# Linear attention with a gated feed-forward layer on one core: the second batch's q and k transposed by the DMA, half loads, and tail groups that keep their PSUM tile, in a new order

## Chip, cores, metric

One core of one Trainium2 chip. The metric is the device time of one execution, in microseconds (us). The profile names the engines PE (TensorE matmul), PEld (its weight loads), DVE (VectorE), ACT (ScalarE), POOL (GpSimd) and SP (SyncE, which here only issues transfers). A run over 1.5% above the fastest of the same kernel is counted as slow; ratios below use the other runs, called fast, alone.

## The reference

```python
# q, k, v: (8, 8, 576, 64) float32; w_phi: (64, 128)
def phi(x):
    proj = x @ w_phi
    proj = proj - max(abs(proj), over the 128 features)
    return concatenate([exp(proj), exp(-proj)])
q_p, k_p = phi(q), phi(k)
kv, z = k_p^T @ v, sum of k_p over the sequence
x = (q_p @ kv) / (q_p @ z + 1e-6)          # per head; heads side by side: (8, 576, 512)
x_prev = x shifted by one row
xk = mu_k*x + (1-mu_k)*x_prev;   xr = mu_r*x + (1-mu_r)*x_prev
out = sigmoid(xr @ w_r) * (relu(xk @ w_k)**2 @ w_v)      # d_ff = 1024
```

(shortened; all results in float32, the kernel's matmuls in bfloat16)

## The kernel before

Work is cut into 32 head pairs (eight batches of four), numbered through. Each pair goes through projections of q and k, row maxima (`nm`, on DVE), their splitting into two bfloat16 halves (`mhl`), a transposition of these on PE (`ps_m`), exponentials, `kv`, numerator and denominator, and `x_sc`. From pair 8 on, `x_sc` is transposed by a DMA on SP's queue into `xs` (`xz` below), copied by POOL for the shift (`xu`), differenced (`df`) and mixed into `xk` and `xr`. The feed-forward layer of a batch (ps_h, ps_r, ps_v; ps_he, ps_re, ps_ve for the rows that two batches share) then fills PE. The last 64 rows of each head form "tail groups", one for each batch (three for batch 0). A list of names, `ORDER`, fixes the program order of every engine; a name's suffix picks its engine or PSUM slot.

```python
def tr(p0, p1):                                  # q and k of two pairs, transposed by the DMA
    def f():
        t = get(qkT, b, inp, [128, NP * R, 128], BF, "qkT")
        nc.sync.dma_start_transpose(out=t[:, R * p0:R * p1, :],
                                    in_=nat[b][:, p0:p1, :].rearrange("p a x -> p (a x)"))
    return f
...
NPT = 2                                          # batches transposed by PE instead
lparts = {b: [(0, NP)] for b in range(B)}        # whole loads ...
lparts[0] = [(0, 1), (1, 2), (2, 4)]
lparts[1] = [(0, 2), (2, 4)]
...
# tail group: ps_e has two banks, [:, 0] for k and [:, 1] for q
def mte():
    s["pm"] = pm = motile(("mo", "m" + tag), "ps_me")       # a single bank of its own
    nc.tensor.transpose(pm[:, 0:64].bitcast(BF), mh, ident)
def kae():                                                  # add the row maxima of k
    nc.tensor.matmul(s["ps"][:, 0, 0:n * 128], lhsT=s["mT"][0:64, :], rhs=sel[...],
                     start=False, stop=True, skip_group_check=True)
def qte():
    s["pq"] = ps = motile(("mo", "q" + tag), "ps_qe")       # another single bank
    ...
def eqe():                                                  # exponentials tq, out of s["pq"]
    ...
def xz():
    nc.sync.dma_start_transpose(out=xs[:, a, :]..., in_=s["x"]...)
def xu(eng):
    copy(eng, xs[:, a, 1:64], xs[:, a, 576:639])
```

(cuts are marked with dots)

## Time and profile before

| | before |
|---|---|
| time, median of the first 4 runs | 305.4 us (304.2 to 306.4) |
| span of the profiled run | 304.2 us |
| PE / DVE / ACT / POOL busy | 92 / 79 / 73 / 42% |
| first matmul of the feed-forward layer | 51.9 us |
| transposes of xs by the DMA, landing | 3.5 us in the median, 13.4 at most |

The busy shares are averages. Where time is lost is read from the 40 slices, and from "useful work": the number of matmuls of each kind in a stretch times the pitch at which that kind runs when nothing holds it up. The prediction below derives those pitches and shows the lines; in 130 to 140 us the kernel before does 4.8 us of such work, elsewhere after 60 us 8 to 10.

### The profile page before, as it was taken

What the parts mean: (1) busy time and instruction counts of PE and PEld (TensorE: products, weight loads), DVE (VectorE), ACT (ScalarE), POOL (GpSimd) and SP (SyncE); (2) the same over time, 40 slices, a digit from 0 to 9 for tenths busy, and PEclk for the clock granted to TensorE, in tenths of its full rate; (3) what the DMA queues carried; (4) which work ended last, traced back from release to release, by engine and by line L of the source; (5) the groups of instructions that cost most, each with busy time, mean ns of one, the idle gap of its engine ahead of it and who ended that gap; (6) DMA issues with size and microseconds to landing.
All of it is one profiled execution on the core that took longest, in us unless ns stands there. A gap on an engine that the chain in (4) does not pass through costs nothing.

```text
span 304.2 us, 9054 instructions
## 1 busy us (share of the span) xinstructions
PE 278.4 (92%) x3765; PEld 158.4 (52%) x3813; DVE 240.3 (79%) x369; ACT 223.3 (73%) x408; POOL 127.4 (42%) x261
## 2 busy tenths in 40 slices
PE   6688798999899999969999997999999999999993
PEld 2456465565456655534555654454556655554541
DVE  5776789979978999667978988799869888777331
ACT  3397899998689897855888884898797878923410
POOL 7763533696047346653443714353034403400400
PEclk9999989999999999998999999999999999999999
DMA  8999957399989957996957898913924364233125
GB/s 152 204 209 207 169 83 105 59 194 206 194 174 128 148 124 131 197 200 113 177 110 107 145 125 157 162 47 61 187 60 69 11 93 94 58 74 71 39 58 116
DMA packets 66137, 38.18 MB, mean 126 GB/s; under 512 B 47024, under 2 KB 60720, under 8 KB 66096
## 3 DMA queue, kind: packets, MB, share of 16 engines
q1 hardware_dynamic: 51280, 20.82, 39.4%
q0 software_dynamic: 14672, 16.48, 35.1%
q8 instruction: 30, 0.49, 0.7%
q10 hardware_dynamic: 144, 0.29, 0.3%
q14 instruction: 11, 0.09, 0.1%
HBM read 33.62 MB, written 9.44 MB: 142 GB/s over the span
## 4 chain that ended last, share of the span: by engine, by line
PE 61%; DVE 18%; DMA 7%; ACT 6%; issue 3%; POOL 2%; SPq 1%; DVEq 0%; POOLq 0%
PE ps_v L812 14%; PE ps_h L779 13%; PE ps_r L798 7%; PE ps_nd L656 5%; DMA xs<-x_sc 4%; PE ps_kv L635 4%; DVE nm L565 4%; DVE nm L560 3%; DVE xk L706 2%; PE ps_ve L896 2%; ACT q L620 2%; PE ps_he L866 2%; DVE xr L706 2%; PE ps_q L548 2%; PE ps_k L598 2%
## 5 line engine op out<-in xcount | busy, mean ns | idle before, releaser
L620 ACT ACTIVATE q<-ps_qT 128x512 bf16<-128x512 f32 x128 | 67.1, 622 | 3.0 <-PE ps_qT L612 2.8
L575 ACT ACTIVATE k<-ps_k 128x1024 bf16<-128x1024 f32 x64 | 62.9, 1038 | 5.6 <-PE ps_k L598 4.3
L779 PE MATMUL ps_h<-xk,wk_bf 128*128 128x512 bf16 x237 | 60.8, 379 | 1.3 <-issue 0.3
L812 PE MATMUL ps_v<-wv_bf,kk 128*128 128x512 bf16 x243 | 58.2, 379 | 1.0 <-issue 0.3
L565 DVE TENSOR_REDUCE nm<-ps_q 128x8 f32<-128x1024 f32 x32 | 38.7, 1218 | 4.3 <-PE ps_q L548 4.1
L560 DVE TENSOR_REDUCE nm<-ps_k 128x8 f32<-128x1024 f32 x32 | 38.8, 1217 | 3.8 <-PE ps_k L548 3.8
L812 PEld LDWEIGHTS <-kk 128*128 128x128 bf16 x256 | 23.9, 98 | 28.8 <-issue 1.9
L211 POOL TENSOR_TENSOR kk<-krelu 128x512 bf16<-128x512 bf16 x23 | 23.9, 1047 | 35.4 <-DVE krelu L205 21.7
L779 PEld LDWEIGHTS <-wk_bf 128*128 128x128 bf16 x256 | 22.5, 97 | 25.2 <-issue 2.3
L584 POOL CAST mhl<-nm 128x16 bf16<-128x16 f32 x32 | 8.0, 250 | 64.1 <-DVE nm L560 64.0
L798 PE MATMUL ps_r<-wr_bf,xr 128*128 128x512 bf16 x118 | 32.9, 394 | 1.2 <-issue 0.5
L804 ACT ACTIVATE rt<-ps_r 128x512 bf16<-128x512 f32 x32 | 19.5, 609 | 18.0 <-PE ps_r L798 15.7
L700 POOL TENSOR_TENSOR diff<-xs 128x576 bf16<-128x576 bf16 x21 | 28.0, 1336 | 7.6 <-DVE xs L682 2.8
L203 ACT ACTIVATE krelu<-ps_h 128x512 bf16<-128x512 f32 x39 | 23.2, 611 | 10.1 <-PE ps_h L779 8.3
L706 DVE SCALAR_TENSOR_TENSOR xk<-diff,mu_k_t,xs 128x576 bf16<-128x576 bf16 x32 | 28.5, 892 | 1.3 <-POOL diff L700 1.0
L818 DVE SCALAR_TENSOR_TENSOR ob<-rt,ps_v 128x512 f32<-128x512 bf16 x32 | 21.8, 682 | 8.7 <-PE ps_v L812 4.2
L666 DVE TENSOR_TENSOR x_sc<-ps_nd,rden 128x640 bf16<-128x640 f32 x32 | 26.4, 825 | 1.1
L706 DVE SCALAR_TENSOR_TENSOR xr<-diff,mu_r_t,xs 128x576 bf16<-128x576 bf16 x32 | 26.9, 840 | 0.0
L548 PEld LDWEIGHTS <-qkT 64*128 64x128 bf16 x512 | 17.6, 94 | 12.0 <-issue 9.7
L635 PE MATMUL ps_kv<-v,k 64*128 64x65 bf16 x1024 | 22.8, 192 | 0.6 <-ACT q L620 0.4
L635 PEld LDWEIGHTS <-k 64*128 64x128 bf16 x1024 | 19.9, 95 | 5.1 <-issue 3.8
L205 DVE TENSOR_SCALAR krelu<-ps_h 128x512 bf16<-128x512 f32 x25 | 17.1, 688 | 6.6 <-PE ps_h L779 6.0
(99 smaller groups left out, 467.5 us busy)
## 6 DMA issues: line engine op xcount, KB each, us to landing
out_dram<-ob SPq DMA_DIRECT2D x72, 128.0 KB, 2.4
nat<-in_k_dram POOLq DMA_DIRECT2D x6, 576.0 KB, 8.6
nat<-in_q_dram POOLq DMA_DIRECT2D x6, 576.0 KB, 8.9
vt<-in_v_dram POOLq DMA_DIRECT2D x6, 576.0 KB, 9.6
wk_bf<-in_moe_w_k_dram POOLq DMA_DIRECT2D x2, 512.0 KB, 10.8
wv_bf<-in_moe_w_v_dram POOLq DMA_DIRECT2D x2, 512.0 KB, 12.3
nat<-in_k_dram POOLq DMA_DIRECT2D x3, 288.0 KB, 7.4
nat<-in_q_dram POOLq DMA_DIRECT2D x3, 288.0 KB, 7.3
```

Of the source, the lines that this page charges most:

```text
L211: (nc.vector if eng == "DVE" else nc.gpsimd).tensor_tensor(out_, in_, in_, op=ALU.mult)
L560: nc.vector.tensor_reduce(s["nm"][:, 0, :], s["k"].rearrange("p a (g f) -> p (a g) f", f=128), axis=AX.X, op=ALU.max, apply_absolute_value ...
L565: nc.vector.tensor_reduce(s["nm"][:, 1, :], s["q"].rearrange("p a (g f) -> p (a g) f", f=128), axis=AX.X, op=ALU.max, apply_absolute_value ...
L575: nc.scalar.activation(s[f"k{pn}"], s["k"].rearrange("p a (g f) -> p (a g) f", f=128), AF.Exp, scale=(1.0 if pn == 0 else -1.0))
L620: nc.scalar.activation(t[:, h, :].rearrange("f (g a p) -> f g a p", g=4, a=2), s["qT"].rearrange("f a (g h p) -> f h g a p", g=4, h=2)[:, ...
L635: nc.tensor.matmul(ps[:, hh, pn * 65:(pn + 1) * 65], lhsT=s[f"k{pn}"][r, c, :], rhs=vb[r, a, 2 * g + par, :], start=(pn == 0 and c == 0), ...
L666: nc.vector.tensor_tensor(s["x"].rearrange("p (b s) d -> p b s d", b=2), ndv[:, :, :, 0:64], s["rd"].to_broadcast([128, 2, 5, 64]), op=ALU ...
L700: (nc.vector if eng == "DVE" else nc.gpsimd).tensor_tensor(s["d"], xs[:, a, 64:64 + S], xs[:, a, 0:S], op=ALU.subtract)
L706: nc.vector.scalar_tensor_tensor(out=t[:, a, (b % 2) * S:(b % 2 + 1) * S], in0=s["d"], scalar=mu[:, a:a + 1], in1=xs[:, a, 0:S], op0=ALU.m ...
L779: nc.tensor.matmul(ps, lhsT=wk_bf[:, c, fc * 128:(fc + 1) * 128], rhs=xkt[bp][:, c, m0:m0 + 512], start=(c == 0), stop=(c == NDC - 1))
L798: nc.tensor.matmul(ps, lhsT=xrt[bp][:, c, m0 + ci * 128:m0 + (ci + 1) * 128], rhs=wr_bf[:, c, :], start=(c == 0), stop=(c == NDC - 1))
L812: nc.tensor.matmul(ps, lhsT=s["kk"][:, fc, ci * 128:(ci + 1) * 128], rhs=wv_bf[:, fc, :], start=(fc == 0), stop=(fc == NFC - 1))
```

## The change

The intent: free PE, DVE and ACT of the second batch's transposes at the start; keep large loads away from the transposes of x (a half load below brings two of a batch's four pairs); give the tail groups fewer PSUM banks to wait for. The order of nearly everything is new as well.

```diff
-    NPT = 2
-    lparts = {b: [(0, NP)] for b in range(B)}
+    NPT = 1
+    lparts = {b: [(0, 2), (2, 4)] for b in range(B)}
...
+        pace = lambda i: [f"xu{4 * (b - 3) + i + (a0 > 0) * (1 if i > 3 else 2)}"] if b > 4 else []
-            op(f"lk{tag}", "POOL", 0.75, at("lk"), ld(0), ["ident"], alloc=al("nat"), chain="ld")
+            op(f"lk{tag}", "POOL", 0.75, at("lk"), ld(0), ["ident"] + pace(0), alloc=al("nat"), chain="ld")
...
         def mte():
-            s["pm"] = pm = motile(("mo", "m" + tag), "ps_me")
-            nc.tensor.transpose(pm[:, 0:64].bitcast(BF), mh, ident)
+            nc.tensor.transpose(s["ps"][:, 1, 0:64].bitcast(BF), mh, ident)
...
         def qte():
-            s["pq"] = ps = motile(("mo", "q" + tag), "ps_qe")
+            s["pq"] = ps = s["ps"][:, 1, :]
...
-        op("mh" + N, "POOL", 0.5, (K("mh"), n), mhx, ...)
+        op("mh" + N, "POOL", 0.5, (K("mh"), n), mhx, ..., alt=("POOL", "DVE"))
```

(cut; further: one exponential of 1024 columns in place of two of 512 for q, mixes and row-maxima splits that may run on POOL or DVE, one more buffer for some tiles, the last output in two halves, and a new `ORDER`. The k, q and v loads of batches 5 to 7 are each held until a given `xu` has run, by `pace`.)

## The prediction

> **What bounds the kernel now.** I read the page first (busy shares, the 40 slices), then the busy time by stretches, then the chain that ended last, then the groups of instructions, and last the timeline of the worst gap.
>
> ```profile
> PE 278.4 (92%) x3765; PEld 158.4 (52%) x3813; DVE 240.3 (79%) x369; ACT 223.3 (73%) x408; POOL 127.4 (42%) x261
> ...
> PE   6688798999899999969999997999999999999993
> ...
> PE 61%; DVE 18%; DMA 7%; ACT 6%; issue 3%; POOL 2%; SPq 1%; DVEq 0%; POOLq 0%
> ```
>
> TensorE (PE) carries the time, except in three places: the first seven slices (0 to 55 us), one slice near 135 us, and the last one. But 92% flatters it: records of pipelined matmuls overlap. I therefore price its useful work by pitch, read off the chain: four ps_h matmuls in 0.86 us (0.215 each, 512 columns), 20 ps_nd in 0.64, 16 ps_kv in 0.24, 8 projections in 0.22, 9 ps_pt in 0.62. Times the counts of the groups: the 32 head pairs 75 us, the feed-forward 138 + 17 (the joint rows of two batches), tail groups 7, transposes 7, together 245 us of a span of 304.2. The same pricing of the instructions in each stretch gives the PE time lost there (length less useful work, so the fills that only keep the clock up count as lost):
>
> 0 to 55: 29 us lost. 55 to 130: 8 (0.11 per us). 130 to 140: 5.3. 140 to 290: 14 (0.09 per us). 290 to 304.2: 5.0.
>
> ```profile
> core 0: us, PE busy (x) PEld busy (x) DVE busy (x) ACT busy (x) POOL busy (x), PEclk, DMA share, GB/s
> 0.00:55.00 55.00, 43.49 (x708) 27.34 (x714) 41.96 (x79) 40.91 (x81) 30.29 (x67) 0.97 0.98 164
> 55.00:130.00 75.00, 72.95 (x1070) 42.51 (x1082) 65.75 (x93) 63.05 (x115) 40.23 (x73) 1.00 0.98 154
> 130.00:140.00 10.00, 7.07 (x72) 3.46 (x72) 5.58 (x9) 5.82 (x12) 5.58 (x16) 0.83 1.23 198
> 140.00:290.00 150.00, 145.63 (x1883) 81.13 (x1907) 123.28 (x185) 111.77 (x199) 51.34 (x107) 1.00 0.56 95
> ```
>
> Until 55 us DVE and ACT are about three quarters busy and PE has little to do: the feed-forward, its filler, cannot start before pairs 0 to 3 are mixed and wk has landed (first ps_h at 51.9 us). The chain there goes from DVE reductions to PSUM copies and exponentials, so DVE and ACT work is what counts. At 130 to 140 the timeline shows one slow transfer:
>
> ```profile
> 125.10 13.39 DMA xs<-x_sc
> 138.49 0.05 issue
> 138.55 0.23 POOL xs L199
> 138.78 0.04 POOL xs L682
> 138.82 0.14 POOL mhl L584
> ```
>
> GpSimd (POOL) stands at the copy of xs until that transpose lands. The row maxima of the tail group and of the next pairs (mhlt, mhl) are behind such copies in its queue, and PE waits for them (longest 2.4 us); then PE runs at half clock for 3.4 us. Five loads of 576 KB were issued between 117.5 and 126.9 us, just ahead.
>
> **What the Trainium skill says.** "DMA: Bandwidth & Descriptors", Queues, rings and completion order: each DMA engine takes the queues in turn, a whole packet at a time. So a transpose on one queue shares with big loads on another; the trace agrees in kind: xs transposes land in 3.5 us in the median and in 13.4 behind those five loads. "TensorE: Matmul & The Clock Gate", Part 1: an idle window puts the array at half clock for a window of about 3.4 us; the trace shows two such spells, at 36.6 and at 135 us, 3.4 us each, 1.7 us of work lost in each. "GPSIMD Engine Reference", 4.1 Engine selection: two-input elementwise work is about twice as slow as on VectorE; here it is worse, the same difference of 576 columns takes 1336 ns on POOL and 495 on DVE. "Perfetto Trace Analysis", Identifying the Most-Contended Engine, warns of matmul busy time as I found it: 278 us busy for 245 us of work.
>
> **The change part by part.** Lists and diff show a new order of everything, so I count by kind.
>
> (1) Batch 1 by DMA. Gone: 36 of the 72 ps_pt transposes (36 x 0.067 = 2.4 us of PE) and 8 PSUM copies, on DVE 4 x 0.486 + 2 x 0.418 = 2.8 us, on ACT 2 x 0.587 = 1.2 us. New: two transposes of the kind of which 12 exist (landing 5.4 us in the median, 12.8 at worst). They go out while DMA is saturated (the first 30 us run at 0.93 to 1.2 share), but the weights now come after q and k. At 205 GB/s (slices 3 and 4) q and k of batches 0 and 1 with the first halves of v, 2.9 MB as they are listed, are in at about 16 us; even two slow transposes end near 35 us, when pair 4 wants them, so I call them hidden.
>
> (2) Start as a whole. I multiply the instructions listed before the first ps_h by their row's durations: DVE 36.0 us before and 34.5 after, ACT 37.9 and 34.6 (copies gone, one exponential of 1024 columns for two of 512: 0.13 us saved for each pair, four small copies moved; against it mhl, two DVE operations instead of two POOL ones, for five of six pairs). At the same density (36.0/51.9 = 69% and 37.9/51.9 = 73%) ps_h begins at 49.7 by DVE and 47.4 by ACT. I take 48.5: **3.4 us**. The 29 more fills (68 against 39) should keep the clock up near 36 us, which is inside that number.
>
> (3) The hole at 130 to 140. Half loads, for batches 5 to 7 each held back until a given xs copy has run, leave fewer bytes ahead of a transpose; 15 of 32 mhl and 6 of 10 mhlt go to DVE, so a waiting POOL no longer stops PE. The excess is 5.3 - 0.9 = 4.4 us; I count **4**.
>
> (4) Tail groups write row maxima and q's tail into the second bank of their own tile: 20 uses fewer of the two single banks that ps_h, ps_r and ps_v alternate in, against a three-fold tile held about 1.1 us longer (two tq exponentials). With deeper buffers (kpn, qpn, kvs, krelu, rt, d one more each) this goes at the stretches of 180 to 190 and 200 to 210 us, which lose 2.2 and 1.8 instead of 0.9: excess 2.2 us. I count **2**.
>
> (5) The end. The last joint rows come in two halves of 256 columns, the last output on two queues. Now: ps_ve done at 299.25, ob 0.69, two issues in 1.10, landing. Half of ob and of the issues goes: 0.35 + 0.55 = **0.9 us**.
>
> (6) Costs. Some 18 more load issues of 0.75 us on POOL, 13 us of an engine with 58% idle: off the path, unless a copy of xs waits behind one. Five mixes go to POOL, two operations and over 2 us each, chosen where it has time. For new waits in an order made on a model of the machine I take off 0.7.
>
> Sum: 3.4 + 4 + 2 + 0.9 - 0.7 = 9.6 us, and 305.6 - 9.6 = 296. The parts err rather low, as the lists were searched with more freedom (engines, buffers): I say **295**.
>
> **Rivals.** *A, the hole moves*: batches 2 to 4 are not held back, POOL still runs all xs copies in order, and a slow transpose can stop it elsewhere (33.5 us of its waits are on xs). For: 12 such waits exist, only one hurts PE much. Then parts 3 and 4 give 2 instead of 6: 299. *B, the start is bound by DMA*: the transposes of batch 1 and the later weights hold up pair 4 or ps_h. For: DMA full until 30 us. Against: it falls to 0.6 from 40 us on, before ps_h. Then part 2 gives nothing or costs 2: 298 to 301. *C, DVE becomes the bound*: the lists give it 238 us against 239, so its share hardly moves; against. It would show as 300 and more. *D, denser throughout*: losing 0.07 instead of 0.09 per us over 225 us would give 5 us more: 290.
>
> **Range and chances.** A and B together end at about 302, D at 288; eight in ten lie in 288 to 302. Faster by over 2% means under 299.6: only A with B, or C, miss it, so 0.78; same 0.20; slower 0.02.
>
> **What would show it.** Right: first ps_h at 47 to 50 us; no copy of ps_pt for batch 1, ps_pt x36; no half-clock spell after 10 us; no slice of PE under 9 between 60 and 290; xs landing under 8 us at worst; q exponentials x64 at about 1.04 us. Wrong: PE waiting for qkT by DMA before 50 us (B), PE behind mhl or xs once more (A), DVE above 85% after 60 us (C). The prediction falls if the useful-work pricing shows the loss after 60 us unchanged or grown.

## The result

The kernel after is slower. Its first four runs gave 318.7 us in the median (314.4 and 316.8 fast, 320.5 and 321.9 slow), a ratio to the kernel before of 1.034 [1.024, 1.043]. Run once more beside later experiments it gave 318.8 us (317.0 to 320.2, all fast), ratio 1.041 [1.036, 1.047]:

> The kernel after once more, unchanged, for a profile in the fast state and for times on one chip with the other runs of this call. Theory (x transposes in turn with loads): the same holes at 140 to 150 and 200 to 210 us as in the slow profile, useful work below 6 us in each, POOL's waits for xs over 40 us. Rival (the holes belong to the slow state): they are gone in a fast profile. Time of the fast runs 313 to 317.

The holes are in its fast profile too (3.9 and 3.5 us of useful work), and POOL's waits for xs are 51.1 us; only its time is higher than I said. A ratio is the mean time of one kernel's fast runs over that of the other's of the same rounds, so not quite the ratio of the medians quoted; the interval in brackets is of 95%. The lines below are from the fast profile of that second run.

The page of the kernel after (busy shares, two rows of the slices, the chain):

```profile
PE 284.1 (90%) x3761; PEld 158.4 (50%) x3814; DVE 249.5 (79%) x409; ACT 222.3 (70%) x346; POOL 143.6 (45%) x235
...
PE   8798889998999899977999999198999889999995
...
PEclk9999999999999999995999999789999999999999
...
PE 56%; DVE 21%; issue 6%; DMA 6%; POOL 5%; ACT 4%; SPq 0%; DVEq 0%; POOLq 0%; ACTq 0%
```

The hole that was one slice near 135 us is gone from there, but the 19th and the 26th slice (143 to 151 and 198 to 206 us) are new holes, with the clock halved beside each. The stretches around them, first of the kernel after, then the same ones of the kernel before (columns as in the prediction):

```profile
130.00:140.00 10.00, 9.68 (x164) 5.81 (x165) 9.62 (x16) 8.83 (x14) 5.98 (x7) 1.00 1.13 96
140.00:150.00 10.00, 6.24 (x31) 2.70 (x31) 6.43 (x9) 5.71 (x11) 7.52 (x15) 0.69 1.26 223
200.00:210.00 10.00, 5.10 (x30) 2.11 (x32) 8.16 (x12) 3.04 (x6) 5.13 (x7) 0.66 0.81 98
```

```profile
140.00:150.00 10.00, 9.77 (x115) 4.98 (x113) 9.97 (x13) 6.59 (x11) 5.38 (x10) 1.00 0.74 117
200.00:210.00 10.00, 9.44 (x154) 5.19 (x156) 9.58 (x13) 9.23 (x19) 6.22 (x13) 1.00 0.09 19
```

In useful work, in us, summed from the start (matmul counts times pitches, as in the prediction, but without the transposes ps_pt, which the change takes from PE: 4.8 us before and 2.4 after):

| us from start | before | after | difference |
|---|---|---|---|
| 60 | 25.3 | 26.2 | +0.9 |
| 100 | 60.7 | 61.9 | +1.2 |
| 120 | 79.6 | 78.5 | -1.1 |
| 140 | 94.0 | 96.9 | +2.9 |
| 150 | 103.2 | 100.7 | -2.5 |
| 200 | 148.3 | 145.2 | -3.1 |
| 210 | 156.8 | 148.7 | -8.1 |
| 260 | 204.0 | 191.7 | -12.3 |
| 290 | 233.1 | 220.3 | -12.8 |

So the start gained a little, the old hole was filled, and two new holes and a thinner 100 to 110 and 240 to 260 us cost more. How the hole at 200 us comes about is in the chain of the kernel after, in order of time (start, length, what):

```profile
190.32 8.14 DMA xs<-x_sc
198.47 0.05 issue
198.52 0.24 POOL xs L210
198.76 0.04 POOL xs L692
198.80 0.07 issue
198.87 1.28 POOL diff L709
200.15 0.02 issue
200.18 1.57 DVE xk L720
201.75 1.14 DVE xr L720
202.89 1.14 DVE nm L573
204.03 0.02 issue
204.06 0.37 DVE mhl L597
204.43 0.02 issue
204.45 0.18 DVE mhl L598
```

and in the timeline, DVE's and PE's first work after it (in brackets: idle before, and who ended it):

```profile
200.18 1.57 DVE L720 SCALAR_TENSOR_TENSOR xk<-diff,mu_k_t,xs 128x576 bf16<-128x576 bf16 x1 [8.02 <-POOL diff L709]
```

```profile
204.68 0.29 PE L602 MATMUL ps_m<-ident,mhl 128*128 128x128 bf16 x1 [6.47 <-DVE mhl L598]
```

A slow xs transpose holds POOL's copy and difference; DVE stands 8 us at the mix that needs the difference; the row maxima of k of the next pair (nm) and their split (mhl) are behind that mix in DVE's own queue; PE waits 6.5 us for mhl. The hole at 140 us is the same with POOL in DVE's place. POOL's timeline there:

```profile
140.74 0.24 POOL L210 COPY xs<-xs 128x63 bf16<-128x63 bf16 x1 [4.62 <-DMA xs<-x_sc]
...
141.26 0.76 POOL L329 DMA_DIRECT2D nat<-in_k_dram  x1 [0.25 <-issue]
142.04 1.28 POOL L709 TENSOR_TENSOR diff<-xs 128x576 bf16<-128x576 bf16 x1
143.27 0.19 POOL L483 CAST mhlt<-me 128x4 bf16<-128x4 f32 x1
143.53 0.70 POOL L484 TENSOR_TENSOR mhlt<-me,mhlt 128x4 bf16<-128x4 f32 x1
```

The tail group's mhlt, for which PE waits 3.5 us, stands behind the copy of xs, and also behind the issue of a half load (0.76 us) that was put right behind that copy and a difference (1.28 us).

The waits in total (us, times, longest), three lines of the kernel after, then one of before:

```profile
POOL xs L210 <- DMA xs<-x_sc: 51.1, 17, 8.7
PE ps_m L602 <- DVE mhl L598: 9.5, 5, 6.5
PE ps_e L495 <- ACT tq L517: 4.8, 5, 1.2
```

```profile
POOL xs L199 <- DMA xs<-x_sc: 33.5, 12, 7.5
```

POOL waits for xs more, not less. The last line of the first three did not exist before at all: PE's addition of row maxima to a tail group (ps_e) waits about 1 us, five times, for the tq exponentials. Two theories follow: **loads** (the new places of the loads make the transposes slower) and **shared tile** (the tail group's k addition writes a tile that its q exponentials still read).

### The profile page after: what moved, and what is told of

It reads as the page before. It is cut to its first block, busy times and chain, and to the rows that moved or that the text cites.

```text
span 320.1 us, 9003 instructions
## 1 busy us (share of the span) xinstructions
PE 282.9 (88%) x3761; PEld 158.0 (49%) x3814; DVE 247.7 (77%) x409; ACT 222.5 (70%) x346; POOL 144.3 (45%) x235
## 4 chain that ended last, share of the span: by engine, by line
PE 54%; DVE 19%; DMA 10%; ACT 6%; SPq 4%; issue 3%; POOL 3%; DVEq 0%; POOLq 0%; ACTq 0%
PE ps_v L828 13%; PE ps_h L795 11%; DMA xs<-x_sc 6%; PE ps_r L814 5%; PE ps_nd L666 4%; DVE nm L578 3%; PE ps_kv L646 3%; DVE nm L573 3%; SPq L361 3%; PE ps_ve L918 2%; DMA out_dram<-ob 2%; DVE x_sc L676 2%; PE ps_qT L619 2%; DMA nat<-in_q_dram 2%; PE ps_k L611 2%
## 5 line engine op out<-in xcount | busy, mean ns | idle before, releaser
L632 ACT ACTIVATE q<-ps_qT 128x1024 bf16<-128x1024 f32 x64 | 63.0, 1028 | 5.6 <-PE ps_qT L625 5.4
L828 PE MATMUL ps_v<-wv_bf,kk 128*128 128x512 bf16 x241 | 60.2, 387 | 1.4 <-issue 0.5
L222 POOL TENSOR_TENSOR kk<-krelu 128x512 bf16<-128x512 bf16 x25 | 26.6, 1066 | 52.4 <-DVE krelu L216 39.1
L720 DVE SCALAR_TENSOR_TENSOR xk<-diff,mu_k_t,xs 128x576 bf16<-128x576 bf16 x29 | 26.5, 914 | 13.5 <-POOL diff L709 13.3
L814 PE MATMUL ps_r<-wr_bf,xr 128*128 128x512 bf16 x116 | 31.8, 386 | 1.1 <-issue 0.4
L210 POOL COPY xs<-xs 128x63 bf16<-128x63 bf16 x23 | 7.4, 320 | 53.4 <-DMA xs<-x_sc 48.1
L214 ACT ACTIVATE krelu<-ps_h 128x512 bf16<-128x512 f32 x36 | 21.5, 601 | 9.0 <-PE ps_h L795 8.8
L709 POOL TENSOR_TENSOR diff<-xs 128x576 bf16<-128x576 bf16 x19 | 25.1, 1323 | 3.4 <-DVE xs L210 1.9
L216 DVE TENSOR_SCALAR krelu<-ps_h 128x512 bf16<-128x512 f32 x28 | 19.3, 688 | 6.6 <-PE ps_h L795 6.4
L646 PE MATMUL ps_kv<-v,k 64*128 64x65 bf16 x1024 | 21.8, 190 | 0.5 <-ACT q L632 0.3
## 6 DMA issues: line engine op xcount, KB each, us to landing
wr_bf<-in_moe_w_r_dram POOLq DMA_DIRECT2D x2, 256.0 KB, 11.2
```

Source lines behind the costliest of these rows:

```text
L222: (nc.vector if eng == "DVE" else nc.gpsimd).tensor_tensor(out_, in_, in_, op=ALU.mult)
L632: nc.scalar.activation(t.rearrange("f j (a p) -> f j a p", a=2), s["qT"].rearrange("f a (j p) -> f j a p", p=64), AF.Exp, scale=(1.0 if pn ...
L646: nc.tensor.matmul(ps[:, hh, pn * 65:(pn + 1) * 65], lhsT=s[f"k{pn}"][r, c, :], rhs=vb[r, a, 2 * g + par, :], start=(pn == 0 and c == 0), ...
L709: pick(eng).tensor_tensor(s["d"], xs[:, a, 64:64 + S], xs[:, a, 0:S], op=ALU.subtract)
L720: nc.vector.scalar_tensor_tensor(out=t[:, a, (b % 2) * S:(b % 2 + 1) * S], in0=s["d"], scalar=mu[:, a:a + 1], in1=xs[:, a, 0:S], op0=ALU.m ...
L814: nc.tensor.matmul(ps, lhsT=xrt[bp][:, c, m0 + ci * 128:m0 + (ci + 1) * 128], rhs=wr_bf[:, c, :], start=(c == 0), stop=(c == NDC - 1))
```

## The experiments

Thirteen kernels ran, the kernel after once more among them. They ran on different chips, so ratios are compared and not times.

### 1 and 2. Loads cut away, in both kernels

```diff
+                if b >= 4:                                    # wrong result on purpose
+                    nat[b] = nat[b - 2]
+                    nc.gpsimd.dma_start(out=nat[b][:, a0:a0 + 1, o:o + 16], in_=heads(...)[:, 0:1, 0:16])
+                    return
```

The k, q and v loads of batches 4 to 7 stay at their places but carry 16 columns of one pair.

> The changed kernel with the loads of q, k and v of batches 4 to 7 cut to 16 columns of one pair (they are still issued at the same places and with the same waits; the result is wrong on purpose). Theory C (contention: a transpose on the SP queue crawls while loads flow, and POOL, then DVE, then PE stand behind the xs copy): the holes near 140-150 and 200-210 us vanish, xs lands in under 6 us at worst, no half-clock spell after 10 us, 293 to 301 us. Rival O (order: the new order itself, its SP queue and its xs copies on POOL alone, make the holes): holes remain, over 308 us.

Measured: 306.6 us, ratio 0.995 [0.987, 1.003]: between the two forecasts.

> The kernel before with the same loads cut in the same way (wrong result on purpose). Theory C: its one hole at 130-140 us goes too, 298 to 302 us; the difference between this and the changed kernel without loads is what the rest of the change is worth (by the prediction some 5 us in favour of the change). Rival O: as before, 304 to 306.

Measured: 301.1 us, ratio 0.978 [0.969, 0.987]. Its hole at 130 to 140 us is gone (8.8 us of useful work in place of 4.8). The holes of the kernel after go too; the same stretches of a_noload:

```profile
140.00:150.00 10.00, 8.77 (x97) 4.30 (x97) 9.85 (x13) 8.20 (x14) 4.65 (x12) 1.00 0.89 162
200.00:210.00 10.00, 9.27 (x127) 5.06 (x122) 9.25 (x14) 8.47 (x16) 4.01 (x13) 1.00 0.61 134
```

The slowest transpose of xs lands in 6.3 us in a_noload, against 9.9. As its issues and SP's queue are those of the kernel after, rival O falls for these two holes. So these loads cost the kernel before 2.2% (some 7 us) and the kernel after 4.6% (1.041 to 0.995, some 14 us; 3.9%, 12 us, with its first ratio of 1.034). But without them the kernel after is still 1.7% behind: the loads are about half of the loss. A hole of another kind is left, at 100 to 110 us (5.0 us of useful work), with the clock halved for 3.4 us from 105.8 us on. PE's longest waits in a_noload, one of them in that hole:

```profile
PE ps_e L503 <- ACT tq L525: 4.8, 5, 1.2
```

### 3. The new code in the old order

The kernel after's code with the order of before (tail groups with single banks again, half loads side by side, the second batch's q and k by the DMA).

> The changed kernel's code (DMA transposes of batch 1, half loads, one exponential of 1024 columns, deeper buffers, split end) in the order of the kernel before: each load replaced by its two halves side by side, the tail groups with their single banks again as that order needs. Theory C and rival O both: the loss sits in the order (for C in where its loads stand), so 300 to 306 us with one hole at 125-139 as before. Rival F (a feature of the code is at fault: half loads or the batch 1 transposes): 308 us and more.

Measured: 322.7 us, ratio 1.049 [1.039, 1.058]: the number that rival F forecast. PE waits for the DMA's q and k:

```profile
PE ps_e L463 <- DMA qkT<-nat: 12.1, 2, 7.4
```

The clock is halved for 17 us from 34 us on, and the useful work at 60 us is 15.5 (25.3 before). In the old order the weights are loaded (issued at 13.9 to 23.9 us) where the second batch's transposes now run: these, issued at 17.1 and 28.6 us, landed at 40.0 and 45.1, against 30.3 and 33.1 in the kernel after. This run shows how they share. Packets of two queues, counted from the trace's DMA records (loads: mostly 1152 bytes, weights 1024; transposes: 256 bytes):

| kernel, stretch | packets of loads | packets of a transpose |
|---|---|---|
| a_border 34 to 36 us | 318 | 316 |
| a_border 36 to 38 us | 307 | 308 |
| before 134 to 136 us | 289 | 274 |
| after 148 to 150 us, no load | 0 | 2141 |

Beside loads that fill the stretch a transpose gets one packet for each packet of a load, 270 to 320 in 2 us; alone it gets up to 2141 (about 1670 in the other stretches that one fills, 124 to 126 or 242 to 244 us for instance). In the kernel after's hole at 192 to 194 us it is 242 packets against 243. Where loads are fewer it gets more: 710 against 164 at 190 to 192 us. A transpose of xs has 640 packets and one of q and k for two pairs 2304, so a pair of the latter, issued beside loads, fills some 30 us (an estimate: 4608 packets at 310 in 2 us). All transposes and output stores are on one queue in order, so an xs transpose also waits for the q and k transposes ahead of it: in the kernel after the two of batch 6 were issued at 178.5 us, beside four half loads issued at 180 to 189 us, and the xs transpose of 190.3 us stood behind them: the second of the two landed at 195.9 us, it at 198.5.

### 4. Only the places of the loads moved

```diff
-... lk5.0 lq5.0 so1.3 ...       (24 half loads of batches 3 to 7, many in bursts)
+... xu10/POOL lk5.0 ... xu11/POOL lq5.0 lv4.0 ...    (no more than two near one x transpose)
```

> The changed kernel with nothing but load issues of batches 3 to 7 moved on the POOL queue, so that at most two half loads stand near one transpose of x and the four of batch 4 come before them all. Theory C: the holes shrink, xs lands under 7 us at worst, 298 to 306 us. Rival O: over 312 us as the changed kernel.

Measured: 308.4 us, ratio 1.002 [0.994, 1.010], against 1.034 to 1.041 of the kernel after. The time lies between the two forecasts, and the slowest xs transpose lands in 8.2 us, not under 7. POOL's waits for xs fall from 51.1 us:

```profile
POOL xs L211 <- DMA xs<-x_sc: 36.6, 14, 7.1
```

The hole at 200 us closes; the one at 140 us shrinks (6.1 us of useful work). Moving load issues, and nothing else, gives 3 to 4%. That is direct support of the first theory, without a wrong result.

### 5. Only the tail groups' additions moved

```diff
-qte3.0 eqe3.0 rk12 mh12/DVE kae3.0 ekt3.0
+qte3.0 kae3.0 eqe3.0 rk12 mh12/DVE ekt3.0        (likewise 0.1, 1.0, 6.0, 7.0)
```

The timeline of PE in the kernel after at one of these places (its previous matmul is 0.71 us late too):

```profile
103.12 0.21 PE L511 MATMUL ps_e<-mTe,sel 64*128 64x128 bf16 x1 [0.71 <-issue]
104.51 0.37 PE L495 MATMUL ps_e<-sel,mTe 64*128 64x512 bf16 x1 [1.17 <-ACT tq L517]
```

In five groups the order puts `eqe` (two exponentials out of bank 1) between `qte` and `kae` (a matmul into bank 0). Before, bank 1's work was in a tile of its own. Now it is the same tile, and the matmul into bank 0 waits until the exponentials have read bank 1.

> The kernel after, with five tokens of the order moved: in the tail groups 0.1, 1.0, 3.0, 6.0 and 7.0 the addition of the row maxima for k (into bank 0 of the tile) is put directly after the q part (into bank 1) and so ahead of the tq exponentials, which it waited for in the profile after (PE ps_e on ACT tq: 4.8 us in 5 waits). Theory (the reuse of one PSUM tile makes the addition wait about 1 us for the exponentials of the other bank, and each wait is on the PE path): the 5 waits of ps_e on tq vanish and the time falls 3 to 5 us against after, to about 313 (fast runs). Rival (those waits lie beside the x transposes' holes and what they take is given back there): the waits vanish and the time stays within 1.5 us of after.

Measured: 315.4 us, of which 312.0 and 313.9 fast, 316.9 and 317.1 slow; ratio 1.022 [1.015, 1.029] against 1.041 [1.036, 1.047], or 1.034 [1.024, 1.043] in the kernel after's first call. The five waits are gone (the profile is of a slow run). That is 1.2 to 1.9%, 4 to 6 us, about the 4.8 us of waits that the profile put there. With two fast runs, and an overlap with the first interval, this run alone does not settle it; experiment 7 does. The two big holes stay.

### 6. Both

> The kernel a_spread (after with only the load issues moved, 308.4 us) with the same five moves. Theory: 303 to 305, the hole of 140 to 150 us shrinks. Rival: 307 to 309, the holes come from waits on POOL and SP and not from these five.

Measured: 303.5 us (302.5 to 306.6, four fast runs), ratio 0.993 [0.986, 0.999]. (Later expectations quote one of its runs, 302.9.) The additions bring 0.9% here, less than in experiment 5 with the second ratio of the kernel after, with intervals that overlap widely.

### 7. Additions moved, loads cut away

> The kernel after with loads of batches 4 to 7 cut to 16 columns of one pair (wrong result on purpose) and with the row-max additions of five tail groups ahead of the exponentials. a_noload took 306.6 us, the kernel before without these loads 301.1. Theory (the rest of the difference is the five waits on the shared PSUM tile): 301 to 303, as before without loads, so that two causes make up the whole loss. Rival (POOL's mixes and its 18 further load issues cost some us too): 304 to 306.

Measured: 298.8 us, ratio 0.977 [0.972, 0.981]. With experiments 1, 2 and 5 this fills a table (ratios to before):

| | loads as placed | loads cut away |
|---|---|---|
| before | 1.000 | 0.978 |
| after | 1.041 | 0.995 |
| after, additions moved | 1.022 | 0.977 |

The two causes add up: 1.9 and 1.8% for the shared tile, 4.6 and 4.5% for the loads. With the kernel after's first ratio, 1.034, it would be 1.2 and 3.9% in its place; each entry has an interval of 0.5 to 1% to either side. The clear step is in the right column, 0.995 [0.987, 1.003] to 0.977: five names moved, and the hole at 100 to 110 us of a_noload is gone (8.3 us of useful work in place of 5.0, clock not halved), so a wait there could also cost a spell of half clock. Without both causes the kernel after is level with before (0.977 and 0.978). So with these loads cut away everything else in the change together is worth nothing to within a per cent.

### 8. Old order, weights behind the transposes

> a_border (after's code in the order of before, 322.7 us), with the loads of the three weight matrices moved behind the transposes of batch 1, where in a_border they ran beside them. Theory (the transposes of batch 1 crawled because their packets took turns with those of the weight loads): ps_k's wait for qkT falls from 12.1 us to under 3, and the time falls by about 15 us to 304 to 309. Rival (the transposes of batch 1 by the DMA are slow or late by themselves): the wait stays at 8 us or more and the time over 315. If it is below 303, the rest of the change's code is worth something in the old order; at 305 or over, it is worth nothing.

Measured: 313.0 us, ratio 1.022 [1.018, 1.026]. No wait for the DMA's q and k is left among PE's longest, and the useful work at 60 us is 25.0, against 15.5 in a_border and 25.3 before. That is the first theory at another place. The time was missed all the same, for a reason of my own making: with half loads side by side POOL issued fourteen transfers (0.7 us each) in 55 to 72 us, and a tail group's mhlt stood behind them:

```profile
PE ps_me L484 <- POOL mhlt L479: 4.9, 1, 4.9
```

The useful work in 60 to 80 us fell from 17.3 to 11.2. From 90 to 290 us it is 182 us in both orders, so the other parts of the new code are worth nothing there either.

### 9. PE transposes put back

The order of a_spread_kae with four `pt` groups in place of the two DMA transposes.

> a_spread_kae (302.9 us) with the second batch's q and k transposed by TensorE again, four groups each ahead of the first projection that needs its PSUM slot, copies on VectorE and ScalarE. The prediction priced the part at 3.4 us gained by the DMA. Theory of the prediction: 305 to 307. Rival (before the expert layer starts the PE path waits for other things, so these transposes lay in idle time): within 1 us, 302 to 304.

Measured: 318.6 us, ratio 1.031 [1.022, 1.040]. Neither expectation held (the fast runs took 313.9 and 317.5 us). I put each group right ahead of the projection that takes over its PSUM slot, so the PSUM copies stood on the chain there; 9.6 us of useful work are missing at 60 us already. It is no clean price of the part, and does not show what the DMA transposes of batch 1 cost; that they hold PE up nowhere is read from the kernel after's trace, where PE never waits for them.

### 10 to 12. Attempts at a faster kernel

b_spread is the kernel before with seven loads moved.

> The kernel before, its code unchanged, with only seven load issues of batches 5 to 7 moved so that no more than two whole loads stand near one x transpose (the burst of five loads at 117 to 141 us is gone). Theory (the hole of 130 to 140 us is three x transposes taking turns with five loads): the hole goes, POOL's waits for xs fall from 33.5 us to under 25, and the time is 300 to 302, near the 301.1 of the kernel before with no such loads. Rival (the hole only moves): 304 to 307.

Measured: 308.8 us, of which 305.4 and 307.2 fast, ratio 1.000 [0.993, 1.007]: the rival. In its profile, of a slow run, the hole moved to 110 to 130 us, where POOL waited for one xs transpose:

```profile
POOL xs L199 <- DMA xs<-x_sc: 7.8, 1, 7.8
```

> a_spread_kae with one x difference (pair 15) on VectorE in place of GpSimd and one half load later. In a_spread_kae one mix on VectorE at 140.9 us took 3.38 us (others 0.81) while GpSimd ran a copy, two load issues, a difference and two copies without a gap. Theory (VectorE was held off by GpSimd's run of operations there, and that is most of the hole of 140 to 150 us): the long mix is gone and the time falls to 300 to 302. Rival: the hole comes from the q and k transposes of batch 5 and stays, 302 to 304.

Measured: 306.1 us over 21 runs, ten fast ones of 300.9 to 305.0 (ratio 0.988 [0.985, 0.992]) and eleven of 306 to 310 counted as slow. The 3.4 us mix is gone and 140 to 150 us does 8.1 us of useful work in place of 6.1, so that part of the theory held, though with two things moved it is not shown which of them did it. The profile, of a slow run, has a new hole at 170 us, and this wait at a load's issue:

```profile
POOL nat L330 <- DMA qkT<-nat: 9.8, 1, 9.8
```

The buffer that the load fills is still being read by the q and k transposes of batch 5.

> a_best with the four half loads of q and k of the last batch issued after the x copies of pairs 18 and 19. In a_best (profile in the slow state) GpSimd stood 9.8 us at the first of these load issues at 163.6 us, because the buffer it fills was still being read by the q and k transposes of batch 5, which crawled beside other loads; PE then waited 5.7 us for GpSimd's mhl and the useful work of 170 to 180 us fell to 3.0 us. Theory (this wait at the load issue makes a_best's slow half of the runs): the wait for the DMA of qkT at a load issue is under 1 us, all runs lie together, and the time is 298 to 302, ratio to before 0.975 to 0.985. Rival (the hole moves on to the next x transposes, as in b_spread): 302 to 306.

Measured: 306.7 us over 22 runs (304.7 to 311.7), ratio 0.998 [0.995, 1.000]. The wait is gone, but the useful work of 180 to 190 us is now 5.4 us: the hole moved on, the rival again. Why a_best had two kinds of runs stays open. The best reliable kernel is a_spread_kae, 0.7% under before.

## Why the prediction was wrong

It said 295 us and faster; the runs say 315 to 319 and slower.

1. **Batch 1 by the DMA, "hidden"**: right. The two transposes landed at 30.3 and 33.1 us, PE has no wait for q and k from the DMA before 50 us, and ps_pt is down to 36. Experiment 3 shows it was right only because the order also moved the weights away; rival B described what happens otherwise.
2. **Start, 3.4 us**: mechanism right, size too large. The first ps_h came at 49.7 us (predicted 48.5), and the half-clock spell at 36.5 us is gone, but the useful work at 100 us was only 1.2 us ahead. With the additions of groups 0.1 and 1.0 moved (a_kae) the first ps_h comes at 47.6 us and the work is 2.7 ahead. So the term that was mis-sized is the tail groups' part of the start.
3. **The hole at 130 to 140, 4 us: the step that failed.** It rested on a reading that was too narrow: three transposes of xs were slow there, not one, and PE's longest wait (2.4 us, to 134.5) stood behind the one issued at 120.5 us, which landed at 131.5, not behind the one shown, which landed at 138.5. And it had two halves. "Leave fewer bytes ahead of a transpose" was false: half loads are as many bytes in all, holding one back until a copy has run sets only its earliest time, and the bursts of four to seven half loads of the new order (93 to 101, 131 to 135, 161 to 165, 180 to 189 us) ran beside transposes; POOL's waits for xs rose from 33.5 to 51.1 us, and the loads cost 12 to 14 us in place of 7 (experiments 1 and 2). "A waiting POOL no longer stops PE" was false too: mhl moved to DVE, but behind a mix that waits for POOL's difference, so the same late transpose now stopped DVE for 8.0 us and PE for 6.5.
4. **Tail groups, 2 us: failed in sign.** I counted banks and how long a tile is held, not the new dependence inside the tile. It cost 1.8% (some 5.5 us) by experiments 1 and 7, 1.2 to 1.9% by experiment 5.
5. **The end, 0.9 us**: right. From the last ps_ve matmul to the end of the span it took 4.9 us before (304.2 - 299.25) and 3.8 after (316.9 - 313.05).
6. **Costs, 0.7 us**: the half loads' issues were called "off the path, unless a copy of xs waits behind one". What waited behind one was the mhlt of a tail group, at 141 us.

The prediction had said what would refute it: a loss after 60 us that is unchanged or grown. From 60 to 290 us the kernel after does 194.1 us of useful work, the kernel before 207.8, so it grew by 13.7 us. Of the other signs, "PE behind mhl once more" (A) came; PE waiting for the DMA's q and k (B) and DVE above 85% after 60 us (C; it is 78%) did not.

Rival A (the hole moves) was the right one, but I let it only take back a gain. Holes can also grow: it should have been priced with the loads' full cost on the upper side. And the sum of parts 3 and 4 rested on freedoms of the new order, never on a look at what each transfer would meet.

## What to carry to other kernels

A DMA transpose beside ordinary loads can fall to a fifth or a seventh of its pace (about 300 packets in 2 us against 1670 to 2141), and moving the consumer to another in-order engine doesn't help while something ahead of it on that engine waits for the same transfer; plan loads by what is in flight at their time, not by their size. That is no recipe yet: moving loads brought 3 to 4% in a_spread, but in b_spread and a_best2 the hole only moved. When two banks come to share one tile, list the readers of each and put the writers ahead of them: five reordered names were worth 1 to 2% here. Before blaming one of two suspected causes, remove each and both: the table of experiment 7 left less than a per cent over.

## What the Trainium skill lacked or had wrong

- "DMA: Bandwidth & Descriptors": the turn-taking of queues agrees with these traces, but the page does not say what it means for a transpose beside loads. Here it went one for one in the trace's packets, of 256 against 1152 bytes, where loads filled the stretch, so a transpose fell from up to 2141 packets in 2 us to 270 to 320.
- "TensorE: Matmul & The Clock Gate": the table in Part 1 puts the half clock after at least one idle window of about 3.4 us. In the kernel before a spell of 3.4 us began at 135.5 us although PE's longest idle time there was 2.4 us; in a_noload one began at 105.8 us after idle times of 1.5 and 1.2 us. (Further on, under "A second HAM failure mode", the page reports a kernel where frequent short idles were enough.) The lengths agree: 3.4, 6.8, 10.2 and 17.1 us, all multiples of 3.4.
- No page that I read says that a program's matmul into one bank of a two-bank tile can be made to wait for reads of the other bank, as it was in five places here (4.8 us in all). The trace shows that the program asks for it: each of the five matmuls carries a wait for the semaphore that the second tq exponential raises. What the chip would do without that wait, no run tells.
